# A residual block's convolutions: storing the upper and the lower half of the image side by side

## The chip, the cores and the metric

The kernel runs on one NeuronCore of one Trainium2 chip. The metric is the device time in microseconds of one launch; a comparison uses the median of several runs. Engines are named as in the profile: PE (matmul), PEld (PE's weight load), DVE (vector), ACT (scalar), POOL (GpSimd), SP (the queue that issues most DMAs).

## The reference

A residual block of a diffusion model: x is 2 images of 512 channels, 64 × 64 pixels, in bf16.

```python
h = conv3(silu(gn(x, g1, be1)), w1)          # gn: 4 groups of 128 channels
h = h + (silu(t_emb) @ w_emb).reshape(B, C, 1, 1)
h = conv3(silu(gn(h, g2, be2)), w2)          # conv3: 3 x 3, 512 -> 512, zero padding
return x + h
```

## The kernel before

**Layers, chunks, units.** Channels lie on the 128 partitions in four tiles (ct). A chunk c = 0 to 7 is one layer, one image and one half of that image; chunks 0 to 3 are layer 1, 4 to 7 layer 2. For each chunk four products (c, ct) are made from the input, one for each input tile, and four units (c, k), one for each output tile, consume them. The two convolutions are computed by a short-filter algorithm over rows: the 32 rows of a half are sorted by their number modulo 4 (order FO = 3, 1, 2, 0) into four planes of 8 rows, and sums and differences of planes stand in for rows, so that fewer matmuls are needed. Within a row the even columns come first (32), then a zero, then the odd ones (32): a row has 65 elements (RW), a plane 520 (PL), and a chunk with one halo row above and below 34 rows, 2210 elements (AF).

**One product.** `load_a` brings the 34 rows (layer 1 from x, layer 2 from the scratch h_scr in device memory: one large DMA of 32 rows, one small DMA of the one halo row that lies in the other half, and a POOL memset for the halo row outside of the image). `silu` applies group norm's scale and bias and the silu on ACT, over 33 rows of 64. Then come `k{c}{ct}`, a copy times 4 of 2145 elements (KF; on DVE for chunks 0 to 2, on ACT after that), and `rows_a` and `rows_b` (names row… and rob…), sums and differences of two planes at a time on DVE. From chunk 1 on, `rows_b` ends with the same trick over columns for some of the planes ("nested" kinds: differences of the even and odd columns, in rows of 32 that lie 65 apart; `outer_kinds` does it for two more planes of chunk 7).

**Matmuls.** `plain_mms` makes three matmuls per plane and input tile, one for each column offset kx; each has 512 moving columns, read as 8 rows of 64 at a pitch of 65 (for kx = 1 as 8 rows of two runs of 32). The nested planes give matmuls of 256 contiguous columns (`A_mms`, `B_mms`, C and D). ACT takes the results out of PSUM (`evac_o` writes rows of two runs of 32 at a pitch of 65), and DVE and accumulating DMAs on POOL's queue do the output transform. In layer 1 the results go to h_scr, in layer 2 to the output, on which x was copied before.

**Start.** Layer 1's statistics are made first. For image 0, tile ct, `stats0` (names st00 to st03) uses ones matmuls for sums, and for squares either bn_stats on DVE or matmuls and ACT; a small DVE step on 128 × 128 elements at line 1194 (the gram step) and a chain of small instructions on DVE, PE and POOL end in the scale and bias that silu00 to silu03 need. Eleven and more `fill` matmuls of 512 contiguous columns stand in PE's queue before the first real ones. The weights of layer 1 are combined on DVE too (w1_0 and so on, 1536 elements each). In chunk 0 the first matmuls of ct run as soon as row0{ct} is there, before rob0{ct}. `stats1` (st10 and so on) then loads image 1 for its statistics into ZST.

**Memory.** One fp16 arena `ar` holds nearly all, at offsets written out by hand. Chunk 0's K copies go to three buffers in turn:

```python
WB = [o + 16640]                 # ct 0 and 3
WB += [Z, Z + 6528]              # ct 1, ct 2
ZST = Z + 2176                   # stats1's load of image 1
rows_a(0, ct, WB[ct % 3], CFG["k0"][ct], True)
```

The K copy in Z is 2145 long, so it ends before ZST.

**Order.** Every operation is recorded in a `Plan` with the regions it reads and writes, and then emitted in the order of the string ORDER (two characters per operation), which was worked out ahead for this very list of operations. Each engine's queue runs in that order; semaphores follow from the regions. Most instructions are recorded in helpers, so their lines are the helpers': `tt` 348, `ts` 352, `act` 371, `dma` 386, `memz` 390, `mm` 401 (in the kernel after, three lines less).

Of the kernel before, what the change touches and what calls it, by code (L numbers as in the profile page):

```python
# [115 lines left out]
def _idx(off, dims):  # L116
# [6 lines left out]
FO = (3, 1, 2, 0)  # L123
RW = 65
PL = 8 * RW
YF = 4 * PL
AF = 34 * RW
VP = 4160
KF = 33 * RW
# [39 lines left out]
    "0R0M000O0N2g0P0T0S0Q0p010U020304050607080o0V1J0n1G0e0m1H0k0t0f0l1I0q0s0r0g0u1L1K1M0v0w0h0x1N0y1O0X1P2Z1Q0z0-250Y"  # L169
    "0_2W0i0j1R160Z1a1k3P1S0b1T1l101m190W22121n3X1o2C111U2D1d0a1p2p090A0B0C0D0E0F2F0G0H0I0J0K0L1q132E1r1V141s2G2H1t4t"  # L170
    "1C1u3R2I1W152h2J1v2K1w172L1X2M1x3S181D0d1A1F1B2N3Q1Y1y2O1Z1z1b1-2P4Y1E1c1_1e2s1f4g3U202Q21282S233Y2R2429262T271g"
    "2r2c2U2v2V3T2X1h2d2B2Y0c2a2j2b1i2k2A2y2l1j2z3t2i2m2e2-2o4b2u2q2_2f303n2n313k4a323Z333a3u2t4Z343v3b353c364h2x3738"
    "3d2w393e3C3A3f3m3w3q3B3x453D3g5c3F463h4i3E474d3W5U4k484j493V3i4A4c3G4B4l4C3H3y3K4m4F3p3z3I4G3J6Y3j4H3l4n4I3o4J5W"
    "4f4u4x4K3L4L5X5d4M3r3M51424o3-523_4r4O535V4p544e3s554z564D6Q4-4N574E584s4w6l5B5e5C4q6Z5D5g406m5E415F5Y6n5G5h5H85"
    "5I6S5i5f5p4y435k4v5q865r4P6R5s875u5j5v4Q4T4_5wBK4RBL5x503N4S5y5Z4U5z5-445m4V5l5_5J6T995K625A6a63595n64BM5L3O655o"
    "676c685M5P5a696b5N6d6A5OBO6B666eBa9A6C5t7u6f6V6D5Q6E6o4W6g5R6U6p6h6q8y9B6r6kBN6j6t616u6vBSBPBc6w6xBQ606y6zAD6-6F"
    "73Bb6iBT6G746WBR5b6XAE4X75AF5S76BH786H79777A7B6I6L7C7D7EBeBU7F7J6JBIBW6K7KDI6s6M7LDQBd7cBVBg7M6N6_7d70Bf7N7eBJDR"
    "7G7OBh7f725T7gBY7PBX7Q7hBZ7i7j887k7H7l7m897nDJ7R7o718A7p7S7q7IDT8B7rDS7s7T8DDK8E8F7tDU7v8G8HDM8IEr8JDW8KDY8P7U8Q"
# [24 lines left out]
    "T-TWT_TkU0TXU2U3U4TYU5U6T3U7W2TmU8STU9UBUATnUCTlToUDTZW3UvUETpTqUGUHV8UITcUJTrUKTaULUMTsTbW4UNURUSUwTtUTUUUVUWUX"
    "TuUYWHUaUbU1TdUcXEUdUOUeUfWIUgUyUhTeV9UZUxVAUiUzVBUQXFU-VCUPUFVEV0W5VFVGVHU_VIVJTfVKUjXGVLVNVOV1VPUkXTW6V4VQUlVS"
    "VTVUV3VVUmYSVWVXVMVYVZUoVdW8VeVaVfVgW7VhViUnVjW9YQVkVmVRVnUpYRVoWAVpVqVDVrVsV2UqVtVlWLZ-VcWMVuWBWNWCXHWOVbXVWQWD"
    "WRWSWTVvWUWVXIWWWXWZWFWaVwYTWbZhbDXKWcVxXUWeWfXJWgWYWhWiWEYiWjZfUrWkWlVzV-WpXLWqVyWrZzWsWGWmWtWuWvV_ZgWwWyXMWzW-"
    "WPW_XOW0X0WdX1YkX2XNWxX3XXWnXYX4XPXZXRYUXaYlXSXcXdXeWoXfZiXgXhYWXiXjXlX5XmXkYVXnZxX6auW1XoYXXqYjXrXQXsXtXuYYXvX7"
    "awXwavXxYaX_X8Y0Y1YZX9Y2Y3Y4XyXAY5YbY6Y8Y9YcXbYAYBZjYCXBcYYDYEYFYmYdXCYnXpZyYoYGX-YpZkY7Yrc9Zlc7YsYtYuXzYvYwYeYx"
    "YyY-YzYHY_ZmZ0YIZ1c8ZnYMZ3YJZ4Z5ZpZ6YLZ7doZ8ZoYKZ9ZAZEZBbAYNZFZGZHZIaxZJZKZrYOZLZNZOZCZPZQXDZqZRZSZTYqZDZUZMZ_Yg"
    "a0ZsZVf4a1Z2YPZWa2aybCa4a5Zva6a7a8ZXa9aAcAbBaBa-aDZtaEa_aFa3azaGZbb0ZYaIcQaJaKb1ZaaLaMaNb2ZZaOaPaCZwaTf3aUb3aVaW"  # L210
    "aQaXb5aYaZaaaHaccPadZcaecBafagahaiajb6ZdbEaSabbFcDbGakcCbHcEbJaRbKbLbMcFbNb4bObPbQalZebSbTcHbUdgambVcGaqbXanbYbZ"
    "dpbacKbbapbcbdaobebibRbjYfdhbkarblbmbnbfbobpb8brasbsbqcXbtcJbubvbwcLbxbycZbzYhcacbcUccbhcdbIcecfb9cgcibgcjatckcR"
    "clcmb-cncocpctcqcuZucvcwb_cxchcyczcWc-cVbWc0d0d1d2cIc2d3d4d5cSc1d6cTd7c3cOdAdBcNdCcMdDdEb7dFc4dGdHdMdNdOdPcsc_c5"
    "dQdRdScrexdTd8dqdldrdsdndtdIdudidvdmdVdwdxeydkdzdJdjd-d_d9dUe0e1e2dyc6e3e4dLe8e9dXe5eAeBdKeCeDdYeEeFeHdWdaeIeJeK"
    "dZdbeLeMdceNeOeReSeTeUdeeGeVe7eWeXeYePe6edeeefezegeaf0eheiddeZejgCeQekdff5elf6f7emf8gDf9ecfAe-fBfCf2fEfDebfFfGf1"
    "fHh6e_fIfJeofKfLfPenfMfQfRepfSfTfUesfVereqfWfYfZetfafbfcfdfeffevfXfieufjfkfNewflfgfmfOfnfofpfufhfrfvfwfqfxfyfzf-"
    "fsf_g3gEg1gFgGg4g0gHgIgJg7gKg6g5gLftgNgMgOg8gPgQgRgSgTg2gUgYgVgZg9gagbgAgcgdgWgBgegfghgXgggigjgkglgmgngogrgpgsgq"
    "gtgug_gwh0gxh3h2h1gyh5gzh4g-h7gvh8h9hChAhDhB"
# [3 lines left out]
def kernel(  # L222
# [26 lines left out]
    Z = o + 2528  # L249
# [869 lines left out]
    for i in range(2):  # L1119
        memz("gpsimd", A(AB[i] + 32, [[RW, 34], [1, 1]]), "az")  # L1120
# [270 lines left out]
```

## Time and profile before

| what | value |
|---|---|
| runs | 459.40, 459.79, 459.79 us; median 459.79 |
| profiled execution, span | 459.7 us |
| PE busy | 448.6 us, 98% of the span |
| DVE busy | 436.9 us, 95% |
| ACT busy | 401.8 us, 87% |
| POOL busy | 58.1 us, 13% |
| data moved by DMA | 92.49 MB, on average 201 GB/s |

The profile shows one execution. Its span, from the first to the last instruction, is the only time of that execution that is shown, and it lies within 0.1 us of the median. Busy time of PE counts a matmul from its start to its modelled end; neighbours overlap, so the distance between starts is the better measure of one. "Granted clock" is the share of full speed that the throttle gave PE in a stretch.

### The profile page before, as it was taken

The page shows a single profiled execution, that of the slowest core. Times are in us where ns is not written, and L with a number is a line of the kernel's source. Part 1 is how long each engine was busy: PE and PEld are TensorE (multiplying, and loading weights), DVE is VectorE, ACT ScalarE, POOL GpSimd, SP SyncE. Part 2 cuts the span into 40 slices and gives each one's busy share as a digit, 9 for nine tenths or more (in the row PEclk, how much of TensorE's full clock was granted, in tenths as well). Part 3 has the DMA queues.
Part 4 walks back from the last instruction along what each step waited for, and adds up shares of the span by engine and source line. Part 5 has one row for each costly group of instructions (what it writes and reads, how often), then busy time and mean ns, then how long its engine had stood idle before and what let it go on. Part 6 is the DMA issues. An engine that isn't in the chain of part 4 may idle for free. (4 is left out here: it accounts for less than half of the span.)

```text
span 459.7 us, 8124 instructions
## 1 busy us (share of the span) xinstructions
PE 448.6 (98%) x2904; PEld 282.8 (62%) x2904; DVE 436.9 (95%) x811; ACT 401.8 (87%) x611; POOL 58.1 (13%) x82
## 2 busy tenths in 40 slices
PE   8999999999999999999999999999999999999995
PEld 4754334455555566566665666676666666787882
DVE  2899999999999999999999999999899999999995
ACT  5689999999989999999999999868989869757662
POOL 2110010111111101111000001212121223111220
PEclk9899999999999999999999999999999999999999
DMA  8963561587666468577877947798796989676674
GB/s 321 399 210 109 170 192 47 144 255 223 165 177 202 126 188 233 150 237 217 269 223 234 363 163 229 192 224 222 172 244 156 280 221 260 157 186 122 133 141 93
DMA packets 43176, 92.49 MB, mean 201 GB/s; under 512 B 6400, under 2 KB 18048, under 8 KB 43136
## 3 DMA queue, kind: packets, MB, share of 16 engines
q1 hardware_dynamic: 32208, 77.60, 50.1%
q0 software_dynamic: 10640, 14.38, 20.2%
q8 instruction: 22, 0.36, 0.3%
q14 instruction: 18, 0.15, 0.1%
q10 hardware_dynamic: 288, 0.01, 0.0%
HBM read 62.25 MB, written 31.32 MB: 204 GB/s over the span
## 5 line engine op out<-in xcount | busy, mean ns | idle before, releaser
L401 PE MATMUL psum<-ar 128*128 128x256 f16 (+2 forms) x2771 | 427.7, 316 | 3.3 <-ACT ar L371 2.0
L348 DVE TENSOR_TENSOR ar<-ar 128x1024 f16<-128x1024 f16 (+7 forms) x630 | 413.2, 719 | 8.2 <-ACT ar L371 5.4
L401 PEld LDWEIGHTS <-ar 128*128 128x128 f16 (+1 forms) x2763 | 268.6, 98 | 158.9 <-issue 6.9
L371 ACT ACTIVATE ar<-ar 128x512 f16<-128x512 f16 (+6 forms) x186 | 187.1, 1041 | 26.5 <-DVE ar L348 25.0
L371 ACT ACTIVATE ar<-psum 128x512 f16<-128x512 f32 (+3 forms) x250 | 158.8, 680 | 18.8 <-PE psum L401 10.3
L371 ACT ACTIVATE ar<-ar,fs 128x2112 f16<-128x2112 bf16 (+1 forms) x32 | 68.8, 2154 | 3.7 <-DVE fs L494 3.7
L386 POOL DMA_DIRECT2D ar<-ar x26 | 30.8, 1207 | 218.4 <-DVE ar L348 192.1
L386 POOL DMA_DIRECT2D out_dram<-ar x15 | 18.7, 1244 | 55.0 <-DMA ar<-ar 40.1
L371 ACT ACTIVATION_READ_ACCUMULATOR ar<-psum 128x1 f32 x104 | 22.6, 217 | 0.0
L352 DVE TENSOR_SCALAR ar<-ar 128x520 f16<-128x520 f16 (+3 forms) x50 | 19.6, 404 | 0.0
L390 POOL MEMSET ar<- 128x65 f16 (+4 forms) x29 | 5.8, 269 | 95.1 <-DVE ar L348 48.9
L401 PEld LDWEIGHTS <-ones_bf 128*128 128x128 bf16 x88 | 9.1, 109 | 7.0 <-issue 2.1
L401 PE MATMUL psum<-ones_bf 128*128 128x512 bf16 x32 | 8.8, 438 | 1.1 <-DVE ones_bf L405 1.1
L401 PE MATMUL psum<-ar,ones_bf 128*128 128x260 bf16 x56 | 8.0, 296 | 0.0
L371 ACT ACTIVATION_READ_ACCUMULATOR ar<-ar 128x1 f32 x36 | 7.2, 201 | 0.0
L401 PEld LDWEIGHTS psum<-fs,ones_neg 128*128 128x128 f32 x36 | 4.6, 191 | 2.6 <-issue 1.6
L401 PE MATMUL psum<-fs,ones_neg 128*128 128x1 f32 (+3 forms) x36 | 4.5, 243 | 1.5 <-DVE fs L1130 1.3
L1125 DVE BATCH_NORM_STATS2 fs<-ar 128x6 f32<-128x512 bf16 x4 | 2.5, 681 | 3.7 <-DMA ar<-in_x_dram 3.7
L479 POOL TENSOR_TENSOR fs<-fs 128x1 f32<-128x1 f32 x4 | 3.3, 832 | 19.6 <-DVE fs L477 19.5
L438 DVE CAST fs<-gparm 128x16 f32<-128x16 bf16 x1 | 0.2, 175 | 3.0 <-DMA gparm<-in_params_dram 3.0
L439 ACT ACTIVATE s_sb<-tparm 128x18 bf16<-128x18 bf16 x1 | 0.2, 218 | 3.1 <-DMA tparm<-in_t_emb_dram 3.1
L401 PE MATMUL psum<-ar,s_sb 128*2 128x512 bf16 x9 | 2.7, 377 | 0.0
(54 smaller groups left out, 24.4 us busy)
## 6 DMA issues: line engine op xcount, KB each, us to landing
ar<-in_w_dram SPq DMA_DIRECT2D x36, 384.0 KB, 5.1
ar<-in_x_dram SPq DMA_DIRECT2D x16, 552.5 KB, 4.7
h_scr<-ar SPq DMA_DIRECT2D x16, 520.0 KB, 5.3
ar<-h_scr SPq DMA_DIRECT2D x16, 520.0 KB, 4.7
out_dram<-in_x_dram SPq DMA_DIRECT2D x30, 260.0 KB, 5.8
out_dram<-ar POOLq DMA_DIRECT2D x15, 520.0 KB, 8.0
ar<-in_x_dram SPq DMA_DIRECT2D x13, 520.0 KB, 4.9
u_scr<-ar SPq DMA_DIRECT2D x16, 384.0 KB, 3.8
```

The source lines that it names most:

```text
L348: pl.op("DVE", 0.075 + 0.000521 * out.n, lambda: nc.vector.tensor_tensor(out=out.ap, in0=a.ap, in1=b.ap, op=op), regs(a, b), regs(out), name)
L352: pl.op("DVE", cost or 0.075 + 0.00026 * out.n, lambda: nc.vector.tensor_scalar(out=out.ap, in0=a.ap, scalar1=s, scalar2=None, op0=ALU.mul ...
L371: lambda: nc.scalar.activation(out=out.ap, in_=a.ap, func=func, scale=sc, **kw), regs(*rr), regs(*ww), name)
L386: lambda: eng.dma_start(out=out, in_=in_, **kw), regs(*r), regs(*w), name, lat=3.2 if sw else None, after=after, sw=sw, seq=seq)
L390: pl.op("POOL" if eng == "gpsimd" else "DVE", 0.08 + 0.0005 * out.n, lambda: e.memset(out.ap, v), (), regs(out), name)
L401: nc.tensor.matmul(out.ap, lhsT=lhsT.ap, rhs=rhs.ap, start=st, stop=sp, skip_group_check=True)
L438: nc.vector.tensor_copy(out=fs[:, GB:GB + 4 * CT], in_=gparm[:])
L439: nc.scalar.activation(out=s_sb[:], in_=tparm[:], func=ACT.Silu)
L479: pl.op("POOL", 0.85, lambda: nc.gpsimd.tensor_tensor(out=F(rs, n).ap, in0=N.ap, in1=F(NEGH, n).ap, op=ALU.pow), regs(N), regs(F(rs, n)), ...
L1125: pl.op("DVE", 0.61, lambda: nc.vector.bn_stats(out=q.ap, in_=e.ap), regs(e), regs(q), nm)
```

## The change

A chunk is no longer one half of the image but 16 rows of the upper and 16 of the lower half, and element j of an upper row lies beside element j of the lower row that is 32 further down. A row has 130 elements (RP) where it had 65, a plane has 4 such rows where it had 8 (520 elements as before), and a chunk with its halo rows is 18 rows, 2340 elements. All shifts by one column become shifts by two elements, and runs of 32 or 64 elements become runs of 64 or 128.

Each chunk now has a halo on both sides: one of its halo rows holds, in one of the two interleaved halves, a row outside of the image, and in the other a real row. So layer 2's loads have two small DMAs (130 and 129 elements) where they had one (65), and the zeros are written after the silu, by a POOL memset of 65 elements at a step of two, in each of the 32 products, where 16 memsets of one row stood before the loads. `silu` covers 18 × 128 elements where it covered 33 × 64; the K copy is 2210 elements where it was 2145. The four memsets that clear the two input buffers once at the start become two, over the whole buffers. The arena's offset Z moves by 288, and ZST = Z + 2176 stays, so the K copy in Z now reaches 34 elements past it. ORDER is a new string for the new list. Host code lays x out in this form and takes the output apart again; `yr`, `yo`, `s_ops`, `D_mms` and the statistics read and write the same elements as before by the new strides, and are left out here.

```diff
-RW = 65
-PL = 8 * RW
+RP = 130
+PL = 4 * RP
 YF = 4 * PL
-AF = 34 * RW
+AF = 18 * RP
 VP = 4160
-KF = 33 * RW
+KF = 17 * RP
...
-ORDER = (...)
+ORDER = (...)
...
-    Z = o + 2528
+    Z = o + 2240
...
-            zr = A(ab + (0 if ch == 0 else 33 * RW), [[1, RW]])
-            memz("gpsimd", zr, nm)
-            d = A(ab + RW, [[1, YF]])
-            dma(d.ap, h_scr[b, ct, ch], [K("h", b, ct, ch), zr], [d], P * YF * 2, nm)
+            h3, h0 = h_scr[b, ct, 1 - ch][:, 3 * RP:4 * RP], h_scr[b, ct, 1 - ch][:, 3 * PL:3 * PL + RP]
+            d = A(ab + RP, [[1, YF]])
+            dma(d.ap, h_scr[b, ct, ch], [K("h", b, ct, ch)], [d], P * YF * 2, nm)
+            n = RP - 1
             if ch == 0:
-                d = A(ab + 33 * RW, [[1, RW]])
-                dma(d.ap, h_scr[b, ct, 1][:, 24 * RW:25 * RW], [K("h", b, ct, 1)], [d], P * RW * 2, nm)
+                hs = ((A(ab + 1, [[1, n]]), h3[:, 0:n]), (A(ab + 17 * RP, [[1, RP]]), h0))
             else:
-                d = A(ab, [[1, RW]])
-                dma(d.ap, h_scr[b, ct, 0][:, 7 * RW:8 * RW], [K("h", b, ct, 0)], [d], P * RW * 2, nm)
+                hs = ((A(ab, [[1, RP]]), h3), (A(ab + 17 * RP, [[1, n]]), h0[:, 1:RP]))
+            for d, src in hs:
+                dma(d.ap, src, [K("h", b, ct, 1 - ch)], [d], P * RP * 2, nm)
 
     def silu(c, ct):
         l, b, ch = chunks[c]
         ab = acur[(c, ct)]
-        r0 = RW if ch == 0 else 0
-        dims = [[RW, 33], [33, 2], [1, 32]]
-        act(A(ab + r0, dims), A(ab + r0, dims, BF16 if l == 0 else None), ACT.Silu,
+        dims = [[RP, 18], [66, 2], [1, 64]]
+        act(A(ab, dims), A(ab, dims, BF16 if l == 0 else None), ACT.Silu,
             scale=F(scol(l, b, ct)), bias=F(ncol(l, b, ct)), name=f"silu{c}{ct}")
-
-    two = lambda base, r0, r1: A(base + r0 * RW, [[(r1 - r0) * RW, 2], [1, PL]])
+        memz("gpsimd", A(ab + (0 if ch == 0 else 17 * RP + 1), [[2, 65], [1, 1]]), f"z{c}{ct}")
+
+    G3, G1, G2, G0, D5 = RP, RP + PL, RP + 2 * PL, RP + 3 * PL, 2 * RP + 3 * PL
+    two = lambda base, r0, r1: A(base + r0, [[r1 - r0, 2], [1, PL]])
     SB_, AD = ALU.subtract, ALU.add
 
     def rows_a(c, ct, w, keng, early):
...
         ab = acur[(c, ct)]
         nm = f"row{c}{ct}"
         scal(keng, A(w, [[1, KF]]), A(ab, [[1, KF]]), 4.0, f"k{c}{ct}")

-        tt(two(w, 9, 17), two(ab, 1, 26), two(w, 9, 17), SB_, nm)
+        tt(two(w, G1, G2), two(ab, G3, D5), two(w, G1, G2), SB_, nm)
...
-        X = lambda i: A(xb + i, [[RW, 8 * nf], [1, 32]])
-        for kind, (i, j, op) in enumerate(((32, 33, SB_), (1, 0, SB_), (33, 0, SB_), (33, 0, AD))):
+        X = lambda i: A(xb + i, [[RP, 4 * nf], [1, 64]])
+        for kind, (i, j, op) in enumerate(((64, 66, SB_), (2, 0, SB_), (66, 0, SB_), (66, 0, AD))):
             s0 = vnest(c, ct, kind, 0)
             if kind in (1, 2) and CFG["km"]:
                 if kind == 1:
-                    tt(A(s0, [[vnest(c, ct, 2, 0) - s0, 2], [1, 256 * nf]]), A(xb + 1, [[32, 2], [RW, 8 * nf], [1, 32]]),
-                       A(xb, [[0, 2], [RW, 8 * nf], [1, 32]]), SB_, nm)
+                    tt(A(s0, [[vnest(c, ct, 2, 0) - s0, 2], [1, 256 * nf]]), A(xb + 2, [[64, 2], [RP, 4 * nf], [1, 64]]),
+                       A(xb, [[0, 2], [RP, 4 * nf], [1, 64]]), SB_, nm)
...
-                rhs, ps = A(vo, [[RW, 8], [33, 2], [1, 32]]), Ps(bank, 0, [[1, 512]])
+                rhs, ps = A(vo, [[RP, 4], [66, 2], [1, 64]]), Ps(bank, 0, [[1, 512]])
             else:
-                rhs, ps = A(vo + kx // 2, [[RW, 8], [1, 64]]), Ps(bank, 32, [[64, 8], [-32, 2], [1, 32]])
+                rhs, ps = A(vo + kx, [[RP, 4], [1, 128]]), Ps(bank, 64, [[128, 4], [-64, 2], [1, 64]])
...
-            act(A(OO[s - 4], [[RW, 8], [33, 2], [1, 32]]), Ps(bank, 0, [[1, 512]]), fid,
+            act(A(OO[s - 4], [[RP, 4], [66, 2], [1, 64]]), Ps(bank, 0, [[1, 512]]), fid,
...
-        memz("gpsimd", A(AB[i] + 32, [[RW, 34], [1, 1]]), "az")
-    memz("gpsimd", A(AB[0], [[1, RW]]), "az")
-    memz("gpsimd", A(AB[1], [[1, RW]]), "az")
+        memz("gpsimd", A(AB[i], [[1, AF]]), "az")
...
```

More of the change, by code (lines that the diff above doesn't have):

```diff
@@ L174 @@
[L174 to L178, printed above, removed]
@@ L219 @@
+    "fOgDg8gEfsgFgGgHgMg9gJgNgOgIgPgQgRgSgKgTgXgigVgjgkgYgUglgmgngbgogagZgpgLgrgqgsgcgtgugvgwgxgWgyh0gzh1gdh2h3geh4h5g-gfh6h7"
+    "h9g_h8hAhBhChDhEhFhGhJhHhKhIhLhMhThOhUhPhXhWhVhQhZhRhYhShbhNhchdhghehhhf"
 )
@@ L688, in rows_a @@
         if early:
-            tt(two(w, 0, 25), two(w, 0, 25), two(ab, 9, 17), SB_, nm)
-            tt(v45, two(w, 0, 25), two(w, 9, 17), AD, nm)
+            tt(two(w, 0, G0), two(w, 0, G0), two(ab, G1, G2), SB_, nm)
+            tt(v45, two(w, 0, G0), two(w, G1, G2), AD, nm)
         else:
-            tt(v45, two(w, 0, 25), two(ab, 9, 17), SB_, nm)
+            tt(v45, two(w, 0, G0), two(ab, G1, G2), SB_, nm)
     def rows_b(c, ct, w, seng, early, vacc=False):
@@ L698, in rows_b @@
         s4, s5 = vplane(c, ct, 4), vplane(c, ct, 5)
-        rb = 17 if early else 25
-        tt(two(w, 0, rb), two(ab, 1, 25), two(ab, 9, 17), SB_, nm)
-        t2b = A(w + rb * RW, [[1, PL]])
+        rb = G2 if early else G0
+        tt(two(w, 0, rb), two(ab, G3, G0), two(ab, G1, G2), SB_, nm)
+        t2b = A(w + rb, [[1, PL]])
         scal(seng, t2b, t2b, 2.0, nm)
-        Q = two(w, 9, 0)
-        SS = two(w, 25, 17) if early else A(s5, [[w + 25 * RW - s5, 2], [1, PL]])
+        Q = two(w, G1, 0)
+        SS = two(w, G0, G2) if early else A(s5, [[w + G0 - s5, 2], [1, PL]])
         md = mode(c)
@@ L717, in rows_b @@
             v45 = A(s4, [[s5 - s4, 2], [1, PL]])
-            t0 = two(w, 9, 17)
+            t0 = two(w, G1, G2)
             if vacc:
-                d, t = A(s4, [[1, 2 * PL]]), A(w + 9 * RW, [[1, 2 * PL]])
+                d, t = A(s4, [[1, 2 * PL]]), A(w + G1, [[1, 2 * PL]])
                 dma(d.ap, t.ap, [t, d], [d], P * 4 * PL, f"va{c}{ct}", sw=True, acc=True)
@@ L814, in A_mms @@
             rhs = A(vnest(c, ct, q, s), [[1, 256]])
-            lst.append((Ps(bank, q * 32, [[64, 8], [1, 32]]), w, rhs, ct == 0 and q == 0, ct == CT - 1 and q == 1))
+            lst.append((Ps(bank, q * 64, [[128, 4], [1, 64]]), w, rhs, ct == 0 and q == 0, ct == CT - 1 and q == 1))
         return lst
@@ L1170, in stats0 @@
             for i in range(4):
-                bn_stats(A(XB0[ct] + RW + i * 8 * RW, [[RW, 8], [33, 2], [1, 32]], BF16), F(bst + 6 * i, 6), nm)
+                bn_stats(A(XB0[ct] + RP + i * PL, [[RP, 4], [66, 2], [1, 64]], BF16), F(bst + 6 * i, 6), nm)
         else:
-            ones(XB0[ct] + RW, True, cold[0])
+            ones(XB0[ct] + RP, True, cold[0])
             if CFG["st0"][ct] == "A":
-                act(junk(), A(XB0[ct] + RW, [[1, YF]], BF16), ACT.Square, scale=(sc / HW) ** 0.5, acc=F(mg), name=nm)
+                act(junk(), A(XB0[ct] + RP, [[1, YF]], BF16), ACT.Square, scale=(sc / HW) ** 0.5, acc=F(mg), name=nm)
             else:
-                gram(XB0[ct] + RW, cold[1])
+                gram(XB0[ct] + RP, cold[1])
         ones(XB1[ct], half, 1.0 if half else cold[2])
@@ L1300 @@
                     r0, r1 = i * YF // 2, (i + 1) * YF // 2
-                    dma(out[b, k, ch][:, r0:r1], x[b, k, ch][:, RW + r0:RW + r1], [], [K("o", b, k, ch, i)],
+                    dma(out[b, k, ch][:, r0:r1], x[b, k, ch][:, RP + r0:RP + r1], [], [K("o", b, k, ch, i)],
                         P * YF * 1.4, f"pre{c}{k}", after=ufirst[max(ucnt[0] - CFG["pre"], 0)])
@@ L1329, in _layout @@
     a = {k: np.asarray(v) for k, v in inputs.items()}
[L1330 to L1340 removed]
+    x = a["x"].reshape(2, 4, 128, 2, 2, 4, 4, 32, 2)
+    xp = np.zeros((2, 4, 2, 128, 18, RP), x.dtype)
+    m = np.zeros((2, 4, 2, 128, 4, 4, 65, 2), x.dtype)
+    xt = x.transpose(0, 1, 4, 2, 6, 5, 8, 7, 3)[:, :, :, :, list(FO)]
+    m[..., 0:32, :] = xt[..., 0, :, :]
+    m[..., 33:65, :] = xt[..., 1, :, :]
+    xp[..., 1:17, :] = m.reshape(2, 4, 2, 128, 16, RP)
+    h = xp.reshape(2, 4, 2, 128, 18, 65, 2)
+    h[:, :, 0, :, 0, :, 1] = m[:, :, 1, :, 0, 3, :, 0]
+    h[:, :, 0, :, 17] = m[:, :, 1, :, 3, 0]
+    h[:, :, 1, :, 0] = m[:, :, 0, :, 0, 3]
+    h[:, :, 1, :, 17, :, 0] = m[:, :, 0, :, 3, 0, :, 1]
     def wl(w):
@@ L1359, in _unlayout @@
     import numpy as np
-    y = y.reshape(2, 4, 2, 128, 4, 8, RW)
-    r = np.empty((2, 4, 128, 2, 8, 4, 32, 2), y.dtype)
+    y = y.reshape(2, 4, 2, 128, 4, 4, 65, 2)
+    r = np.empty((2, 4, 128, 2, 2, 4, 4, 32, 2), y.dtype)
     for i, f in enumerate(FO):
-        r[:, :, :, :, :, f, :, 0] = y[:, :, :, :, i, :, 0:32].transpose(0, 1, 3, 2, 4, 5)
-        r[:, :, :, :, :, f, :, 1] = y[:, :, :, :, i, :, 33:65].transpose(0, 1, 3, 2, 4, 5)
+        for q in range(2):
+            r[:, :, :, :, :, :, f, :, q] = y[:, :, :, :, i, :, 33 * q:33 * q + 32].transpose(0, 1, 3, 6, 2, 4, 5)
     return np.ascontiguousarray(r.reshape(2, 512, 64, 64))
```

156 lines of the change are left out of this document (73 added, 83 removed).

## The prediction, made before the run

> **What bounds the kernel now.** I read the busy shares first, then the same shares by stage, because an average hides which engine is the limit where.
>
> ```profile
> PE 448.6 (98%) x2904; PEld 282.8 (62%) x2904; DVE 436.9 (95%) x811; ACT 401.8 (87%) x611; POOL 58.1 (13%) x82
> ```
>
> ```profile
> core 0: us, PE busy (x) PEld busy (x) DVE busy (x) ACT busy (x) POOL busy (x), PEclk, DMA share, GB/s
> 26.00:40.00 14.00, 14.00 (x65) 6.21 (x65) 13.71 (x30) 14.00 (x11) 0.93 (x1) 1.00 0.47 169
> 40.00:95.00 55.00, 55.00 (x247) 23.31 (x246) 54.42 (x94) 54.87 (x82) 4.52 (x4) 1.00 0.49 142
> 95.00:150.00 55.00, 55.00 (x316) 30.90 (x315) 53.23 (x115) 51.26 (x100) 4.83 (x5) 1.00 0.69 204
> 150.00:260.00 110.00, 109.30 (x691) 67.31 (x689) 109.62 (x206) 108.11 (x224) 7.07 (x13) 1.00 0.70 217
> 260.00:455.00 195.00, 191.88 (x1427) 139.13 (x1425) 188.77 (x314) 156.91 (x177) 35.39 (x41) 1.00 0.78 194
> ```
>
> From 26 us on PE has about 4 us of gaps in 429 (14 + 55 + 55 + 109.3 + 191.9 = 425.2). So a delay of PE's first real matmul reaches the end whole. Up to 95 us, and again from 150 to 260, ACT and DVE are also within about 2% of full; there a faster PE alone gains little. From 95 to 150 ACT has 3.7 us free, and in layer 2 38 us.
>
> The third view is the timeline of the start (start, length, engine, line).
>
> ```profile
> 15.01 4.19 ACT L371 ACTIVATE ar<-ar,fs 128x2112 f16<-128x2112 bf16 x2 [3.71 <-DVE fs L494]
> 17.70 1.18 DVE L352 TENSOR_SCALAR ar<-ar 128x2145 f16<-128x2145 f16 x2
> 19.41 0.28 DVE L1194 SCALAR_TENSOR_TENSOR ar<-psum,ident 128x128 bf16<-128x128 f32 x1
> 19.99 2.98 PE L401 MATMUL psum<-ones_bf 128*128 128x512 bf16 x13
> 20.23 0.72 DVE L352 TENSOR_SCALAR ar<-ar 128x2145 f16<-128x2145 f16 x1
> 24.29 0.83 PE L401 MATMUL psum<-ar 128*128 128x512 f16 x3
> 24.82 0.39 ACT L371 ACTIVATE ar<-psum 128x260 bf16<-128x260 f32 x1 [1.42 <-DVE ar L1194]
> 26.04 8.17 PE L401 MATMUL psum<-ar 128*128 128x512 f16 x36
> ```
>
> silu00 and silu01 run from 15.01 to 19.20; DVE makes k00 from 17.70; at 19.41 it does st02's gram step, which ACT and then PE wait for; k01 follows at 20.23; PE starts convolving at 24.29 and never stops after 26.04.
>
> **The start: DVE's order.** The orders of instructions of the two programs are the same on PE and ACT. On DVE, besides two copies in layer 2 that find their data ready, one block moves: k01, row01 (three) and rob01 (four) now stand directly after st01's last step (16.70), ahead of the last product of w1_0's first part, k00, row00 and st02's gram step. The layout asks for it: the buffer of ct 1 begins at Z and is now 2210 long, and the first stats1 load begins at Z + 2176, so that load must wait for rob01. In before rob01 runs only at 36.9 to 42.8.
>
> DVE is in order, so k01 blocks it until silu01 has ended and its halo is zeroed. silu01 ends at 19.2 + 0.2 (x loads 6% longer) + 2 × 0.16 (silu, below) = 19.7, the memset takes about 0.26 with its two waits, so k01 starts at 20.0 and DVE stands idle 2.2 us from 17.8. Then, by the durations of before: k01 and three row01 2.98, rob01 2.3, to 25.3; w1_0's product, k00, another product and row00's first step 2.6, so st02's gram step is at 27.9 in place of 19.4. ACT waits for it (st02's square is done by 21.5) and ends the chain at 28.6; PE does the mean chain 28.7 to 29.4, eight ones matmuls, then its first convolving matmuls at 30.3 (before 24.29). ACT does st03's square 28.6 to 30.5; after it the second gn chain lets PE's long run start at 32.2 (before 26.04). That is 6.0 and 6.2 us late.
>
> PE meanwhile has nothing from the end of the fill (23.0) to 28.7. What 2.6 us with only twelve two-column matmuls do to the clock can be seen earlier:
>
> ```profile
> 11.10:14.50 3.40, 2.40 (x23) 2.30 (x24) 2.38 (x13) 0.21 (x2) 0.88 (x1) 1.00 1.03 420
> 14.50:17.90 3.40, 3.40 (x27) 2.65 (x24) 3.36 (x9) 2.89 (x2) 0.92 (x4) 0.50 1.03 390
> 17.90:21.30 3.40, 3.40 (x33) 2.43 (x31) 3.40 (x8) 3.40 (x5) 0.00 (x0) 0.99 1.05 391
> ```
>
> One stretch of 3.4 us was granted half. After a gap of 5.7 us I expect the same once: the eight ones matmuls 0.8 us longer and the next three up to 0.3, of which some hides under ACT's square; 0 to 1.1, taken 0.6. Start: **+6.8** (6.2 to 7.3). [...]
>
> **PE's row breaks.** The 512-column matmuls read 8 rows of 64 at a pitch of 65; now 4 rows of 128 at 130.
>
> ```profile
> L401 PE MATMUL psum<-ar 128*128 128x512 f16 x1080 | 249.7, 386 | 0.5 <-ACT ar L371 0.4
> ```
>
> In the long run of 36 the starts are (8.17 − 0.39)/35 = 222.4 ns apart, in the fill (2.98 − 0.38)/12 = 217; over the whole trace 222.5 against 215.7 for contiguous data. So the breaks cost 6.8 ns. With half as many rows I take 3.4 ns × 1080 = 3.7 us (0 if the cost is by the column shift, 7.3 if it is by starts at odd elements). By stage: chunk 0 (288 matmuls) 1.0, chunk 1 (192) 0.65, chunks 2 and 3 (288) 1.0, layer 2 (312) 1.06. Chunk 0, 2 and 3 lie where ACT and DVE are full: nothing granted. Chunk 1 and layer 2: **−1.7**. The matmuls of 256 columns read contiguous planes before and after: nothing.
>
> **DVE's nested differences.** Rows of 32 at 65 become rows of 64 at 130. By the groups of two short windows, the op of 2048 elements in such rows (at 341.7) took 1287 ns, a contiguous one (at 338.3) 1218:
>
> ```profile
> L348 DVE TENSOR_TENSOR ar<-ar 128x2048 f16<-128x2048 f16 x1 | 1.3, 1287 | 0.0
> ```
>
> ```profile
> L348 DVE TENSOR_TENSOR ar<-ar 128x2048 f16<-128x2048 f16 x1 | 1.2, 1218 | 0.0
> ```
>
> That is 69/64 = 1.1 ns per row; 3328 rows cost 3.6 us, half is 1.8 (all 3.6 if odd starts cost it). 2304 of the rows are layer 2's, half of their cost 1.2, and there DVE ends some of PE's 3.1 us of gaps: **−1.1** (0 to −2.5). [...]
>
> **ACT.** silu covers 18 rows of 128, 2304 elements, in place of 2112:
>
> ```profile
> L371 ACT ACTIVATE ar<-ar 128x2145 f16<-128x2145 f16 x20 | 40.2, 2008 | 1.7 <-DVE ar L348 1.4
> ...
> L371 ACT ACTIVATE ar<-ar,fs 128x2112 f16<-128x2112 bf16 x16 | 34.2, 2145 | 3.7 <-DVE fs L494 3.7
> ...
> L390 POOL MEMSET ar<- 128x65 f16 x18 | 4.3, 274 | 80.3 <-ACT ar L371 45.7 <-DVE ar L348 34.6
> ```
>
> The K copy of 2145 elements takes 2008 ns and a copy of 512 takes 623, so a column is 0.85 ns; 192 more are 0.16 us, ×32 = 5.2, and twenty K copies 65 longer add 1.1. Layer 2's share lies under 38 free us. From 26 to 95 ACT gets six silus, 1.0 us against 0.13 free: it eats what PE would have won in chunk 0. From 150 to 260 it gets 1.5 against 1.9 free. Price beyond that: 0 (to +0.9).
>
> **The zero memset and the halo loads.** A POOL memset now stands between each silu and its K copy: 0.26 us. Where K on ACT follows silu within 0.2 us, or DVE's first row op follows K within 0.4, it shows: some ten places, **+0.6** (0.2 to 1.5). POOL is in order, but in all 32 places it is free before the silu ends (nearest: 28.01 against 29.25), so nothing queues behind it. SP issues 16 more small loads (260 bytes per partition): in layer 2 these go two units ahead, hidden; uncovered, one costs the 0.33 us that an issue takes.
>
> **Sum.** 459.7 (the profiled span, beside a median of 459.79) + 6.8 − 1.7 − 1.1 + 0.6 = **464.3**.
>
> **Rivals.** (A) My case: 464.3, own range 462.3 to 466.5; chance 0.54. (B) The halved breaks are granted in every stage, since DVE has rob01 behind it and PE's start is only 6.2 late: 459.7 + 6.2 − 3.7 − 1.1 = 461.1, down to 460.3 if more gaps of layer 2 close. For: DVE is only 4.4 us late after the start. Against: ACT at 54.87 of 55. 0.17. (C) The pitch was never the cost; spacing stays 222.5, the DVE rows too, and ACT becomes the limit up to 95 us: 459.7 + 6.8 + 0.9 + 0.6 = 468.0. For: the form with two runs of 32 per row costs the same as the one with 64, so the number of runs isn't it. 0.13. (D) The other side: all 6.8 ns go because every row now starts at an even element; layer 1 was limited by PE, and ACT's fullness is only waiting work: 459.7 + 6.2 − 7.3 = 458.6. It decides when the spacing falls below about 216.5. For: kx 2, shifted by one element, is 1.5 ns dearer than kx 0. Against: contiguous pieces that start off 16 bytes cost only 3 ns. 0.12. [...] 0.04.
>
> **Numbers.** Likeliest A: 464.3. Range 459.4 to 468.0: it leaves out the lower part of D and the upper half of C and E. Faster by over 0.2% (below 458.9), about what the measurement can tell: three quarters of D, 0.09; within 0.2%: the rest of D and the lower third of B, 0.09; slower 0.82.
>
> **What would show it.** k01 at 20.0 right after an idle of 2 us on DVE; st02's gram step near 27.9; PE's first 512-column matmuls on ar near 30.3 and the long run near 32; a granted clock of about 0.5 once near 28 to 32; spacing near 219 ns; silu 2.31 us; then PE as full as before. Wrong if the long run starts before 29, or if PE's span from there to the end shrinks by more than 4 us.

## Result and the profile after

The change made the kernel slower: 470.15 us median of 5 runs (468.84 to 470.65) against 459.79; ratio 1.0217, 95% interval 1.0201 to 1.0233. That is 10.4 us, where 4.5 were forecast. A launch mostly takes 1.7 to 2.1 us more than its span (470.15 with a span of 468.1). The execution of before that the profile shows was itself a long one: in other runs of before the span was mostly 457.7 to 458.1, with times of 459.5 to 459.9, so it is by accident that its span of 459.7 lies near the median time. In comparing the two traces 1.8 us must therefore be added to what they differ by (8.4).

The stages after, in the columns of the windows view:

```profile
core 0: us, PE busy (x) PEld busy (x) DVE busy (x) ACT busy (x) POOL busy (x), PEclk, DMA share, GB/s
26.00:40.00 14.00, 11.43 (x42) 6.40 (x43) 10.34 (x29) 9.97 (x12) 1.72 (x4) 0.63 0.70 246
40.00:95.00 55.00, 55.00 (x255) 24.05 (x254) 51.71 (x87) 54.44 (x72) 3.56 (x8) 1.00 0.43 140
95.00:150.00 55.00, 54.86 (x313) 30.37 (x311) 53.62 (x117) 52.55 (x101) 5.49 (x8) 1.00 0.70 200
150.00:260.00 110.00, 108.00 (x688) 67.14 (x687) 109.10 (x208) 109.50 (x217) 8.67 (x16) 1.00 0.68 209
260.00:455.00 195.00, 189.79 (x1427) 139.15 (x1426) 190.34 (x317) 164.24 (x194) 34.77 (x42) 1.00 0.81 210
```

PE's gaps from 26 us on went from 4 to 10 us. 2.6 of them belong to the start, but from 150 on they grew, too, from 3.8 to 7.2, although PE has less to do. The start, by the timeline of the kernel after:

```profile
19.78 0.74 DVE L349 TENSOR_SCALAR ar<-ar 128x2210 f16<-128x2210 f16 x1 [2.87 <-POOL ar L387]
...
27.65 0.29 DVE L1190 SCALAR_TENSOR_TENSOR ar<-psum,ident 128x128 bf16<-128x128 f32 x1
...
28.04 0.39 ACT L368 ACTIVATE ar<-psum 128x260 bf16<-128x260 f32 x1 [6.61 <-DVE ar L1190]
...
28.57 1.44 PE L398 MATMUL psum<-fs,ones_neg 128*128 128x2 f32 x6 [5.64 <-ACT ar L368]
...
29.87 1.89 PE L398 MATMUL psum<-ar,ones_bf 128*128 128x260 bf16 x8
...
31.56 1.49 PE L398 MATMUL psum<-ar 128*128 128x512 f16 x3
...
33.98 6.35 PE L398 MATMUL psum<-ar 128*128 128x512 f16 x19
```

k01 stands first, and DVE waits 2.87 us until silu01 has ended (19.51) and its zeros are written; the gram step comes at 27.65 (forecast 27.9), PE has a hole of 5.6 us as forecast. But then each small group on PE takes 1.8 to 2 times as long as in before (six two-column matmuls 1.44 us in place of 0.72, eight of 260 columns 1.89 in place of 1.05, three of 512 1.49 in place of 0.83), and the long run starts at 33.98, 7.9 us late, where 6.2 were forecast. The windows show why:

```profile
24.70:28.10 3.40, 0.00 (x0) 0.00 (x0) 3.40 (x8) 0.06 (x1) 0.00 (x0) 0.98 0.56 189
28.10:31.50 3.40, 2.93 (x14) 2.47 (x15) 2.32 (x5) 2.33 (x4) 0.00 (x0) 0.50 0.95 310
31.50:34.90 3.40, 3.40 (x14) 1.98 (x12) 1.65 (x10) 2.48 (x5) 0.99 (x2) 0.50 0.87 299
34.90:38.30 3.40, 3.40 (x10) 1.20 (x9) 2.61 (x7) 3.40 (x2) 0.72 (x2) 0.51 0.53 214
38.30:41.70 3.40, 3.40 (x18) 1.51 (x17) 3.37 (x6) 3.40 (x4) 0.17 (x1) 1.00 0.45 128
```

Three stretches at half clock, not one. The first has gaps, the second still holds the six two-column matmuls of the last statistics chain; 34.9 to 38.3 is the first that holds nothing but 512-column matmuls, and after it 1.00 was granted.

What PE was to win is there in full. In the kernel after its long run at full clock goes

```profile
38.20 18.10 PE L398 MATMUL psum<-ar 128*128 128x512 f16 x83
```

so (18.10 − 0.38)/82 = 216.1 ns from start to start (215.8 over the trace), as for contiguous data. On DVE the 16 differences of 2048 elements in rows of 64 take 1219 ns on average, the contiguous time; all 63 operations of that size together, 1236 ns in before, now stand at 1220:

```profile
L345 DVE TENSOR_TENSOR ar<-ar 128x2048 f16<-128x2048 f16 x63 | 76.5, 1220 | 5.6 <-ACT ar L368 5.1
```

Both kinds of row break are gone wholly, not by half. And yet: PE's order is the same in both programs, so each matmul can be compared with itself. After the half clock PE is 9.9 us late (at 39 us); its faster matmuls bring that down to 7.2 by 160 us; then there are steps back, +1.1 at 161 us and +1.7 at 278, and from 280 on it stays at 8.1 to 8.8. The two steps are waits, the second one at the join of the two layers, where before waited less:

```profile
160.80 1.46 PE L398 MATMUL psum<-ar 128*128 128x512 f16 x9 [0.91 <-DVE ar L345]
...
278.29 1.91 PE L398 MATMUL psum<-ar 128*128 128x256 f16 x16 [2.77 <-ACT ar L368]
```

```profile
269.57 1.69 PE L401 MATMUL psum<-ar 128*128 128x256 f16 x14 [1.05 <-ACT ar L371]
```

DVE, compared in the same way, is 8.1 to 9.1 late from 82 us to the end (but for the two groups of row steps that changed place). PE regained time and then had to wait for engines that had regained none.

### The profile page after: what moved, and what is told of

Its sections match the earlier page's. It is cut to its first block, busy times and chain, and to the rows that moved or that the text cites. A ratio compares the mean times of both kernels' runs of the same rounds, so it can differ in the third digit from the quotient of the medians.

```text
span 468.1 us, 8191 instructions
## 1 busy us (share of the span) xinstructions
PE 447.1 (96%) x2904; PEld 284.9 (61%) x2904; DVE 439.3 (94%) x811; ACT 407.4 (87%) x611; POOL 63.1 (13%) x96
## 5 line engine op out<-in xcount | busy, mean ns | idle before, releaser
L368 ACT ACTIVATE ar<-ar 128x512 f16<-128x512 f16 (+6 forms) x186 | 189.4, 1059 | 23.2 <-DVE ar L345 21.8
L368 ACT ACTIVATE ar<-ar,fs 128x2304 f16<-128x2304 bf16 (+1 forms) x32 | 74.3, 2324 | 4.4 <-DVE fs L491 4.1
L387 POOL MEMSET ar<- 128x65 f16 (+4 forms) x43 | 10.8, 262 | 207.9 <-ACT ar L368 199.4
L368 ACT ACTIVATION_READ_ACCUMULATOR ar<-psum 128x1 f32 x104 | 24.9, 239 | 0.0
L398 PE MATMUL psum<-fs,ones_neg 128*128 128x1 f32 (+3 forms) x36 | 5.7, 275 | 7.1 <-ACT ar L368 5.6
L398 PEld LDWEIGHTS psum<-fs,ones_neg 128*128 128x128 f32 x36 | 5.8, 236 | 8.5 <-ACT ar L368 6.7
L435 DVE CAST fs<-gparm 128x16 f32<-128x16 bf16 x1 | 3.1, 3104 | 2.8 <-DMA gparm<-in_params_dram 2.8
```

The source lines that it names most:

```text
L368: lambda: nc.scalar.activation(out=out.ap, in_=a.ap, func=func, scale=sc, **kw), regs(*rr), regs(*ww), name)
L387: pl.op("POOL" if eng == "gpsimd" else "DVE", 0.08 + 0.0005 * out.n, lambda: e.memset(out.ap, v), (), regs(out), name)
L398: nc.tensor.matmul(out.ap, lhsT=lhsT.ap, rhs=rhs.ap, start=st, stop=sp, skip_group_check=True)
L435: nc.vector.tensor_copy(out=fs[:, GB:GB + 4 * CT], in_=gparm[:])
```

## Experiments

All ratios are against the kernel before on the same chip (medians 459.63 to 459.88 there); a difference between two experiments is that of their medians.

**e1: the start repaired.** DVE's order of before, and the buffer of ct 1 moved 64 elements down so that stats1's load has nothing to wait for.

```diff
-    WB += [Z, Z + 6528]
+    WB += [Z - 64, Z + 6528]
...
+ORDER = (...)   # k01, row01, rob01 where before has them; row62, row63 too
```

> The kernel after, with the buffer of ct 1 moved 64 elements down, so that its copy of 2210 no longer reaches into the place where stats1 loads, and with DVE's order of before (k01, row01 and rob01 back behind k00, row00 and the gram step). Everything else of the change stays. Theory 1 (the block of ct 1 at the start, with the half clock that follows from it, is the whole loss): PE's long run starts near 26.3 us as in before, the granted clock stays full after 18 us, and the time comes back to 457.5 to 461. Rival (the new layout itself costs: longer silus and copies, the wait for the zero memset): 463 or more, with the long run at 26.3 all the same.

462.81 us, ratio 1.0067 (1.0055 to 1.0079). 7.3 us are gone, and 2.9 stay against the 459.88 of before beside it: between the two theories. PE's long run starts at 25.15 and never waits there:

```profile
25.15 11.17 PE L398 MATMUL psum<-ar 128*128 128x512 f16 x51
```

So the start is the larger part, and the layout costs something of its own, although PE and DVE have less to do. The two groups of row steps in layer 2 (row62, row63) went back together with the block; their share of the 7.3 was not measured apart. Where they stand, PE falls back by 0.3 us in the trace of after (at 368 us).

**e2: only the late start, in before.**

```diff
+ORDER = (...)   # k01, row01 (3), rob01 (4) directly behind st01's last step
```

> The kernel before, with only the block k01, row01, rob01 moved to where the kernel after has it. Layout, silu, loads and memsets are those of before. Theory 1: the long run starts 7 to 8 us later, PE is granted about half its clock for two or three stretches of 3.4 us, and the time is 467 to 470. Rival (the loss is the layout's, and a late start would be made good later): below 463.

468.54 us, 1.0178 (1.0158 to 1.0197): 8.7 us from the order of eight DVE instructions alone, in the old layout. The trace is that of the longest of the four launches (467.01 to 470.54). In it PE was granted 0.50, 0.50, 0.50 and 0.58 in the four stretches from 24.7 to 38.3, and the same matmuls run 9.3 us late up to 160 us and 8.7 to 9.0 after that, to the end: next to nothing is made good.

**e3: PE kept busy through the hole.**

```diff
-        mm([(Ps(5, 0, [[1, 512]]), cone, wide, True, True)], "fill", ...)
+        mm([(Ps(5, 0, [[1, 512]]), cone, wide, True, True)] * (26 if i == CFG["fill"] - 1 else 1), "fill", ...)
```

> The kernel after, with 25 more fill matmuls of 512 columns behind the 13 that stand ahead of the gap, about 5.4 us of work that nobody waits for, so that PE is busy until 28.4. Theory 1a (a part of the loss is the half clock: the slow statistics matmuls of the start hold DVE and ACT up, too): the clock stays full from 28 to 38, DVE's first copy of ct 2 starts near 36 in place of 37.4, and the time falls by 1.5 to 3.5 us, to 466.5 to 468.5. Rival 1b (PE's half clock is made good by its faster matmuls, and what sets the end is DVE's order alone): 469.5 to 470.5.

468.31 us, 1.0183 (1.0170 to 1.0196), 1.8 below the kernel after: theory 1a. Windows and timeline of e3:

```profile
28.10:31.50 3.40, 2.90 (x21) 1.87 (x19) 3.27 (x9) 3.13 (x7) 0.63 (x1) 1.00 0.97 298
```

```profile
31.98 8.36 PE L398 MATMUL psum<-ar 128*128 128x512 f16 x38
...
35.62 0.74 DVE L349 TENSOR_SCALAR ar<-ar 128x2210 f16<-128x2210 f16 x1 [1.03 <-POOL ar L387]
```

With the clock held, the long run starts at 31.98 (forecast 32.2). So the order's walk was right to a quarter of a microsecond, and the clock was its mis-sized part: in after the half clock also slowed the small statistics matmuls for which ACT and DVE wait (six in 1.44 us and eight of 260 columns in 1.89, where e3 has 0.83 and 1.05).

**e4: PE's row breaks alone.** In before the 512-column matmuls read 512 contiguous elements; the column offsets are left out.

```diff
-                rhs, ps = A(vo, [[RW, 8], [33, 2], [1, 32]]), ...
+                rhs, ps = A(vo, [[1, 512]]), ...
-                rhs, ps = A(vo + kx // 2, [[RW, 8], [1, 64]]), ...
+                rhs, ps = A(vo, [[1, 512]]), ...
```

> The kernel before, with the 512-column matmuls reading 512 contiguous elements of the plane in place of rows of 64 at 65 (so the column offsets are left out of the convolution). Everything else is that of before. It prices the row breaks alone: the spacing falls from 222.5 to 215.8 ns, 7.2 us on PE in all. If DVE and ACT set the pace from 160 us on, at most 2.5 us of them reach the end: 457 to 459.5. If PE set it: 452.5 to 454.

460.10 us, 1.0001 (0.9993 to 1.0010): nothing, even less than if DVE and ACT set the pace from 160 us on, so neither range held. The spacing did fall (48 matmuls in 10.52 us, 215.7 ns), and PE, 98% busy in before, was not what set the time. Its gaps from 26 us on grew from 3.8 to 9.9 us, nearly by what it saved: the gap at the join of the two layers is 1.05 us in before and 2.26 in e4.

```profile
25.82 10.52 PE L401 MATMUL psum<-ar 128*128 128x512 f16 x48
...
268.14 5.37 PE L401 MATMUL psum<-ar 128*128 128x256 f16 x36 [2.26 <-ACT ar L371]
```

Three of e4's ten launches were granted the full clock throughout and took 458.88 to 459.71, so up to 1 us may be left of PE's 7.

**e9: DVE's row breaks alone.** In before, the nested differences read contiguous planes (other values).

```diff
-        X = lambda i: A(xb + i, [[RW, 8 * nf], [1, 32]])
+        X = lambda i: A(xb + i // 32 * 256 * nf, [[1, 256 * nf]])
...
```

> The kernel before, with DVE's nested differences reading contiguous planes in place of rows of 32 at 65 (the values are not those differences). It takes 3.6 us off DVE by the rows of the trace. e4 took 7.2 us off PE and nothing off the time; if DVE sets the pace, 1.5 to 3.5 us reach the end: 456.4 to 458.4. If ACT and DVE's waits on ACT set it: 459.2 to 460.0.

458.38 us, 0.9970 (0.9955 to 0.9985): 1.4 us reach the end, at the weak end of what a pace set by DVE would give. By the trace the changed instructions took 3.3 us less together (3.6 by the count of rows).

**e5, e6, e8: three costs of the layout, each taken out of e1.**

```diff
-        memz("gpsimd", A(ab + (...), [[2, 65], [1, 1]]), ...)       # e5
+        memz("gpsimd", T(zt[:], ("zt",)), ...)
-        dims = [[RP, 18], [66, 2], [1, 64]]                         # e6
+        dims = [[RP, 17], [66, 2], [1, 62]]
-            for d, src in hs:                                       # e8
+            for d, src in hs[1 - ch:2 - ch]:
```

> The repaired kernel (e1), with the 32 zero memsets written to a small tile that nobody reads, so that the K copy no longer waits for one; the halo elements outside of the image keep what silu made of them. e1 is 2.9 us over before though PE's long run starts no later. If the memset's two waits (0.26 us each) carry it: 1.0 to 2.5 us off, 460.3 to 461.8. If the longer silus do: 0 to 0.7 off, 462.1 to 462.8.

461.44 us, 1.0032 (1.0016 to 1.0048): 1.4 off, as the first reading had it.

> The repaired kernel (e1), with silu over 17 rows of 2 x 62, 2108 elements, nearly the 2112 of before, in place of 2304; the elements left out stay without scale, bias and silu. ACT does 5.2 us less. If ACT carries the 2.9 us that e1 is over before: 1.5 to 3 us off, 459.8 to 461.3. If the memset's waits or the loads do: 0 to 0.8 off, 462.0 to 462.8.

458.54 us, 0.9975 (0.9964 to 0.9986): 4.3 off, more than either theory had, and below before. But the edit takes away more than 5.2 us of work on ACT. The 17 rows leave out a product's last row. In layer 2 the second halo load goes into that row, so the silu no longer waits for it; and in every second product the zeros go there, so they no longer wait for the silu. In the waits of e1, and then of e6:

```profile
POOL ar L387 <- ACT ar L368: 201.4, 30, 23.4
```

```profile
POOL ar L387 <- ACT ar L368: 62.2, 15, 13.2
```

So 4.3 is the most that the work alone can be worth. e14 below gives a least: with memsets and one halo load out as well it comes only 0.6 under e6, where e5 and e8 have 1.4 and 0.7. If those two add, 2.8 is left for the silus. The same holds for e11 and e12, which shorten the silu in the same way.

> The repaired kernel (e1), with the second of the two halo loads of each layer-2 product left out, as many small loads as in before (the halo elements keep older data). If the loads are hidden, as forecast: 462.4 to 463.2. If SP's extra issues or late halos hold back the silus of layer 2 (the steps at 370 us in e1's trace): 1 to 2 us off.

462.15 us, 1.0044 (1.0028 to 1.0059), whose interval touches that of e1: 0.7 off, between the two readings and not clearly told from none. In e1's trace there is one late load, for the silu of a chunk-7 product; ACT stood still for 4.4 us and PE lost 1.6 within the next 6:

```profile
367.15 2.31 ACT L368 ACTIVATE ar<-ar,fs 128x2304 f16<-128x2304 f16 x1 [4.39 <-DMA ar<-h_scr]
...
370.42 1.91 PE L398 MATMUL psum<-ar 128*128 128x256 f16 x16 [0.72 <-ACT ar L368]
```

It was not a halo load. SP issued that product's two halo loads at 352.47 and 354.42, and they had landed by 356.1; the one that was missing is its large load, issued at 357.08 between 260 KB copies from x to the output:

```profile
ar<-h_scr SPq DMA_DIRECT2D x1, 520.0 KB, 10.0
```

In e5, e6 and e8 the same load took 5.2 to 6.4 us, and the two steps on PE at 370 to 373 are missing. What the second halo load does in e1 is to hold up SP's queue, by 2 us: the copy behind it is issued at 354.80, in e8 at 352.74. Whether the large load came late for that reason stays open.

```profile
352.47 2.28 SPq L383 DMA_DIRECT2D ar<-h_scr  x2
354.80 0.52 SPq L383 DMA_DIRECT2D out_dram<-in_x_dram  x1
```

```profile
352.37 0.33 SPq L383 DMA_DIRECT2D ar<-h_scr  x1
352.74 0.51 SPq L383 DMA_DIRECT2D out_dram<-in_x_dram  x1
```

**e12: the short silu in layer 2 only**, on e1.

```diff
+        dims = [[RP, 18], ...] if l == 0 else [[RP, 17], [66, 2], [1, 62]]
```

> The repaired kernel (e1), with the short silu (2108 elements; the rest stays without scale, bias and silu) in layer 2 alone, 16 of 32. With the short silu in both layers 4.3 us went. The forecast had layer 2's longer silus hidden under ACT's 38 free us. If that holds, nearly all of the 4.3 is layer 1's: 462.0 to 462.9. If ACT's order around each product makes them count though ACT is only 81% busy: 460.2 to 461.3.

460.61 us, 1.0012 (1.0002 to 1.0021), the second reading: 2.2 of the 4.3 us come from layer 2. The waits of the stretch from 260 us on (total, times, longest) show where: in e1

```profile
PE psum L398 <- ACT ar L368: 6.0, 9, 2.8
DVE ar L345 <- ACT ar L368: 5.7, 6, 2.3
...
ACT ar L368 <- DMA ar<-h_scr: 4.4, 1, 4.4
```

and in e12

```profile
DVE ar L345 <- ACT ar L368: 4.4, 4, 2.3
PE psum L398 <- ACT ar L368: 3.3, 4, 2.3
...
ACT ar L368 <- DMA ar<-h_scr: 1.2, 2, 0.9
```

ACT is without work for about 37 us there, yet PE and DVE wait for it, and longer where the silus are longer. That a longer silu pushes the evacuation or the K copy behind it, since the queue is in order, fits this but was not tested by itself. Part of the difference is the late load of e1's execution, and part the wait for the second halo load, which the short silu drops; these traces can't separate them.

**e11: the short silu in the kernel after.**

```diff
-        dims = [[RP, 18], [66, 2], [1, 64]]
+        dims = [[RP, 17], [66, 2], [1, 62]]
```

> The kernel after, its late start untouched, with the short silu (2108 elements) in both layers. If the costs add: 4.3 us off, 465.5 to 466.5. If the late start leaves ACT room that takes in part of the longer silus: 1 to 3 us off, 467 to 469.

468.57 us, 1.0184 (1.0161 to 1.0207), whose interval touches that of the kernel after (1.0201 to 1.0233): 1.6 off, the second reading. By the medians the longer silus cost less than half of what they cost in e1 when the start is late.

**e10: a whole kernel with less on ACT.** K copies of chunk 3 on DVE.

```diff
-    'k': ('DVE', 'DVE', 'DVE', 'ACT', ...
+    'k': ('DVE', 'DVE', 'DVE', 'DVE', ...
```

> The repaired kernel (e1), a whole one, with the four K copies of chunk 3 on DVE in place of ACT: ACT 8.3 us less, DVE 2.9 us more, between 150 and 260 us, where both are over 99% busy. By e6 an ACT microsecond was worth 0.8, by e9 a DVE microsecond 0.4: 6.6 less and 1.2 more if the same held in this one stage, but the gain can't be more than the steps seen there (2.8 us): 460 to 462. If DVE is the limit in that stage: 463.5 to 465.5.

467.43 us, 1.0166 (1.0152 to 1.0179), 4.6 above e1: a miss beyond both ends.

```profile
150.00:260.00 110.00, 105.08 (x676) 65.91 (x674) 108.86 (x205) 99.22 (x211) 7.30 (x14) 1.00 0.68 209
```

ACT fell to 99.2 us here and DVE stayed full, which fits DVE as the limit in this stage. Compared with e1 matmul by matmul, PE loses 0.8 us at 160, 1.5 at 190 and 0.7 at 208. The first and the third of these waits end with DVE's work; the second ends with ACT's, and ACT itself had waited 2.22 us for DVE just before:

```profile
187.48 1.15 ACT L368 ACTIVATE ar<-ar 128x512 f16<-128x512 f16 x2 [2.22 <-DVE ar L345]
...
190.10 1.24 PE L398 MATMUL psum<-ar 128*128 128x512 f16 x5 [1.43 <-ACT ar L368]
```

Another 1.5 us come from a stretch at half clock behind the join of the layers, which e1's trace does not have (see the last section). The four copies got new places in ORDER; the rest of it, made for copies on ACT, was not worked out anew.

**e14: all three out at once** (e5, e6 and e8 together, on e1).

```diff
+        memz("gpsimd", T(zt[:], ("zt",)), ...); dims = [[RP, 17], [66, 2], [1, 62]]; for d, src in hs[1 - ch:2 - ch]:
```

> The repaired kernel (e1) with all three costs of its layout taken out at once: the short silu of 2108 elements, the zero memsets aside, and one halo load per layer-2 product (halo elements are left stale, or without scale, bias and silu). What stays of the change is PE without row breaks, DVE without row breaks, and the K copies 65 longer. If these three are all that e1 is over before, the time is that of e9 (before with DVE's row breaks gone), since PE's 7 us brought nothing: 457.5 to 459. If the three add up in full (1.4 + 4.3 + 0.7 off 462.8): 456 to 457. If something else of the layout costs: 459.5 or more.

457.91 us, 0.9964 (0.9952 to 0.9976), within its first range: e9 gave 458.38, with the same rows off DVE and PE as in before. So the three edits together account for what e1 is over before, and PE's 7 us bring nothing on top that the two intervals could tell. No kernel that computes all of the reference beat before.

## Why the prediction was wrong

**Direction and main cause: right.** The ct 1 block ahead of the gram step is the largest part: 8.7 us put into before (e2), 7.3 taken out of after (e1); the forecast had 6.8, up to 7.3.

**The clock: mis-sized.** Forecast 0 to 1.1, taken 0.6; e3 measures 1.8. The step that failed is "I expect the same once": in before the one half stretch was filled from end to end (3.40 of 3.40 us), nearly all with matmuls of 128 and 260 columns, and was the last. Here the first two held gaps or two-column matmuls, and the clock stayed down through both and the next: 0.50, 0.50 and 0.51 were granted, though by the profile's count PE was busy for 2.93, 3.40 and 3.40 of the 3.40 us. That the half clock would end after one stretch was the author's estimate from that single stretch of before; what brings the full clock back was not shown.

**PE's rows: −1.7 forecast, 0 measured** (e4, in before: +0.2, interval of the ratio 0.9993 to 1.0010). The size was wrong on one side, since all 6.8 ns went (as rival D had it), and what is granted of it on the other: chunk 1 and layer 2 were to pass it on. "From 26 us on PE has about 4 us of gaps" was read as "PE sets the time". It does say that PE can't start late without loss (e2), but not that a faster PE ends earlier: in most stages DVE or ACT was as full, and in chunk 1, where ACT had room, the gain was given back at the next join.

**DVE's rows: −1.1 forecast, −1.4 measured** (e9, in before). They went wholly, too: in after the differences of 2048 elements in rows of 64 took 1219 ns and those of 1024 elements 685, as contiguous ones did in before (1219 and 685), where rows of 32 took 1283 and 717.

**ACT: 0 forecast, 2.8 to 4.3 measured in e1 and up to 1.6 in the kernel after.** In e1 this step failed most: "Layer 2's share lies under 38 free us." About half of the 4.3 (2.2) came from layer 2 (e12). The 37 us in which ACT had no work there were not by themselves room for a longer instruction on the path of each product. For layer 1 the forecast set 1.0 us more work against what PE would have won, and 1.5 against 1.9 free us. The first cover was none, as PE's gain was worth nothing; about the second, the other half of the 4.3 says only that some of layer 1's work counted, not where.

**Zero memsets: 0.6 forecast, 1.4 measured in e1** (within the stated 0.2 to 1.5). **Halo loads: hidden by forecast, 0 to 0.7 measured.**

**The sum.** Taken alone, start 8.7, silus 4.3, memsets 1.4, halos 0.7, DVE's rows −1.4 and PE's 0 make 13.7; measured are 10.4. They overlap, as e11 shows for one of them: with the start late, 1.6 of the silus' 4.3 is left, and 8.7 + 1.6 − 1.4 already makes 8.9. The memsets and halos were not measured in the kernel after itself. Against the forecast's terms, the time is 5.9 us over: PE's rows account for 1.7 of that, the silus for up to 1.6, the clock for 1.2, and the memsets and halos, at their price in e1, for 0.8 and 0.7. So no single step explains the miss. That these and DVE's −0.3 come to 5.7 is partly luck, since each is a difference of medians. The base, 459.7, was the span of a long execution, taken for the median of the times; the 1.8 us outside of the span and the 1.8 by which that execution was long cancel, by luck, so this did not shift the forecast.

**Readings that did not move the sum.** DVE's idle time ahead of k01 was put at 2.2 us from 17.8, the end of w1_0's third product; that product stands behind the block, so the idle time began at 16.9. The "two copies in layer 2" are row steps. (8.17 − 0.39)/35 is 222.3. And the memset does not stand ahead of every K copy: in every second product it writes the last row, which the K copy leaves out.

**Rivals.** C came nearest in time (468.0) for a wrong reason: it kept the spacing at 222.5. Its other half, a charge for ACT (0.9, up to 95 us), went the right way, though no run shows the share of that stage. D had the right spacing, and its time fell to the same error as the sum. E (0.04), which had the new rows on DVE dearer than the old ones, did not show: 1219 ns against 1283.

## What to carry to other kernels

When three engines are all 87 to 98% busy under a worked-out order, none of them is the bound by its share: find by one cheap edit each (shorten its work and let the values go) what a microsecond of it is worth at the end; here it was about 0 for PE, 0.4 for DVE and 0.5 to 0.8 for ACT. Check what else such an edit takes away: the short silu also dropped a wait for a load and half of the waits of the memsets. A change of layout also moves the ends of buffers: look for a buffer that now overlaps its neighbour by a few elements, since a scheduler may answer with an order that costs more than the change can bring. And price a hole on PE with the clock that follows: in the kernel after, the hole of 5.6 us was followed by three stretches of 3.4 us that were granted 0.50, 0.50 and 0.51, and in e2 four from 24.7 us on were granted 0.50, 0.50, 0.50 and 0.58.

## What the runs showed of the hardware

- PE: a matmul with 512 fp16 columns read in rows of 64 at a pitch of 65 elements took 222.5 ns from start to start (before), in rows of 128 at 130, where every row starts at an even element, 215.8 (after), also with two runs of 64 per row, and from contiguous data 215.7 (e4). DVE, 2048 elements: 1283 ns on average for 16 ops in rows of 32 at 65 (before), 1219 for 16 in rows of 64 at 130 (after).
- The half clock early in the program differs between executions: 14.5 to 17.9 was granted 0.50 in the profiled execution of before, where PE was busy 2.40 of the 3.40 us ahead of it, and 1.00 in that of e9, whose start is the same code and where it was 3.25. In e9's trace the matmuls of 40 to 95 us run 1.3 us earlier. This is most of the 1.8 us by which the profile of before was long.
- At the join of the two layers PE waited 2.77 us for ACT in after, 2.8 in e1 and e10 and 2.3 in e6 and e12 (before 1.05). From 260 to 455 us the granted clock was 0.99 in e3, e5, e10, e11 and e12 and 1.00 in after, e1, e6 and e14; one stretch of 3.4 us at half clock makes 0.99 of 195 us, and in e10 it lies right behind the hole. In the traces of before and after all changes of the clock are whole multiples of 3.41 us apart. Stretches of that length around the hole (below, e10 first; PE busy, clock, DMA): in e10 it fell into one, with PE busy for 0.62 us, and 0.50 was granted in the next; in e1 into two, with 1.89 and 2.10 us, and none was half; in after, too, into two (1.77 and 2.28 us), and none was. What decides it was not shown: early in before 2.40 us busy were followed by a half stretch. As the one half stretch cost e10 1.5 us, differences of about a microsecond between single traces, or medians of few launches, hold some of this luck.

```profile
269.20:272.60 3.40, 0.62 (x6) 0.99 0.93 344
272.60:276.00 3.40, 3.40 (x16) 0.50 0.12 49
```

```profile
264.20:267.60 3.40, 1.89 (x18) 1.00 1.01 318
267.60:271.00 3.40, 2.10 (x18) 1.00 0.55 223
```

- Two POOL memsets of 2340 elements (2.04 us each, from 3.77) went along with a DVE cast of 16 elements that took 3.10 us in place of 0.17 and ended at 7.88, when the memsets had ended (7.84). It lay beside the wait for x and cost nothing here.
